# Splitting PSUM evacuation and chain copies between ScalarE and VectorE in a decode attention backward kernel

## The chip, the cores and the metric

One core of one Trainium2 chip. The time is the device time of one execution in microseconds, on the slowest (here the only) core. Every kernel was run next to the kernel before on the same chip, and its result was compared with the reference. "Before" and "after" are the two kernels; "span" is the length of the profiled execution, about 1.8 us less than its device time.

Engines: PE is TensorE, ACT is ScalarE, DVE is VectorE, POOL is GpSimd, SP is SyncE. To *evacuate* an outer product means to copy it from PSUM to an SBUF buffer as bf16, from where it is stored to DRAM.

## The reference, cut to what matters

```python
def _fwd(x, k_cache, v_cache, wq, wo, w_gate, w_up, w_down):
    xn = layernorm(x)                       # x: (2, 1, 576)
    q  = xn @ wq                            # 32 heads of 128, 16 KV heads
    p  = softmax(q . k_cache)               # k_cache, v_cache: (2, 16, 4096, 128) bf16
    o  = p . v_cache
    return x + o @ wo + ((B_x@w_gate) * (B_x@w_up)) @ w_down
# the outputs: the result and the gradients of all eight inputs of _fwd for grad_out
```

The caches and weights that must be read are 92.5 MB, and so are the gradients that must be written. The gradient of each cache is a sum of outer products: a row of `p` (or of `ds`, the gradient of the scores) times a short vector. 16 steps go over the caches; in each step, heads of K and V are loaded, K gives scores, V gives `dp`, a chain of small operations (called the *chain* here: `s_sb`, softmax, `ds`, `o_sb`) runs through all engines, and the outer products of the step before are made and stored.

## The kernel before

`# ...` marks a cut.

```python
def ps_m(shape):  return ps.tile(list(shape), FP32, tag="m",  bufs=2)      # PSUM, chains
def ps_sc():      return ps.tile([P, P], FP32,      tag="sc", bufs=2)      # PSUM, scores
def ps_o():       return ps.tile([P, 2, 512], FP32, tag="o",  bufs=2)      # PSUM, pairs of banks

load = {"v": 0.0, "s": 0.0}                 # a cost model, kept while the program is built
def evac(out, in_, cols):
    cv = 0.16 + cols * 0.00104
    cs = 0.19 + cols * 0.00083
    if load["v"] + cv < load["s"] + cs:
        load["v"] += cv
        nc.vector.tensor_copy(out=out, in_=in_)
    else:
        load["s"] += cs
        nc.scalar.copy(out, in_)
def dve(us): load["v"] += us                # other work of DVE, told to the model
def act(us): load["s"] += us

def build_bd(st, b, s, t):                  # block-diagonal operand of the outer products
    # ... two matmuls into bp
    nc.scalar.copy(dense[:], bp[:]);  act(0.4)
    bd = bds[n_bd[0] % 3];  n_bd[0] += 1
    for a in range(4):
        nc.gpsimd.tensor_copy(bd[32 * a:32 * a + 32, :, a, :], dense[32 * a:32 * a + 32])

def by_rows(t_ps):                          # in softmax and in dscores
    nc.scalar.copy(s_sb[:] ..., view(t_ps[:], ...));  act(0.35)
    nc.tensor.transpose(s_ps[:], s_sb[:], identf[:])

def contract(rowsT, heads):                 # p.V and ds.K
    # ... 64 matmuls into o_ps
    nc.scalar.copy(o_sb[:], o_ps[:]);  act(0.3)
    nc.tensor.matmul(t_ps[:], lhsT=o_sb[:], rhs=RV[:] ...)

def outer_units(rows, bd, b, l0, oview):    # eight units for a step's K, eight for its V
    def unit(x, cp):
        # ...
        o = ps_o()
        # ... two matmuls into o
        evac(view(st[:], ...), o[:].rearrange("p c (a d) -> p c a d", a=4), 1024)
        # ... a store of 1 MB after each fourth unit

def softmax(s_ps):
    s_ps = by_rows(s_ps)
    # ... maximum
    nc.scalar.activation(ex[:], s_ps[:], AF.Exp, bias=negb[:], scale=SCALE, accum_out=z[:])

# the last stage: the result, the gradient of x and the gradients of wq (stq, stqt) and wo (sto)
def prepare():
    # ... loads
    nc.vector.tensor_copy(x_f[:], x_b2[:])
    nc.vector.tensor_copy(dy_f[:], dy_b2[:])
    nc.vector.tensor_scalar(xn_f[:], x_f[:], mu[:], None, op0=ALU.subtract)
    nc.vector.tensor_scalar(xn_f[:], xn_f[:], rstd[:], None, op0=ALU.mult)
def gradient():                             # some ten DVE operations on 2 x 576, in a chain
    nc.vector.reduce_sum(m1[:], dxn, axis=AX.X)
    # ...
    nc.vector.tensor_add(dx_bf[:], t1[:], dy_f[:])
```

## Time and profile before

| | before |
|---|---|
| device time, median (range) of 3 runs | 504.05 us (503.95 to 505.25) |
| span of the profiled run, granted PE clock | 501.6 us, 0.879 |
| moved | 186.07 MB, 371 GB/s mean |

The prediction below shows the slices and stretches. From the page, the busy times, and from the table of the costliest groups the evacuations of `so`, the tiles of the cache gradients (columns: line, engine, operation, output and input, count; busy us, mean ns; idle time before them and what ended it), and the copies that build `bd`:

```profile
PE 398.5 (79%) x7417; PEld 266.4 (53%) x7417; DVE 352.5 (70%) x626; ACT 333.7 (67%) x488; POOL 254.2 (51%) x500
...
L112 ACT CAST so<-ps_o 128x1024 bf16<-128x1024 f32 x227 | 221.2, 1023 | 60.6 <-PE ps_o L93 54.2
...
L516 POOL COPY bd<-dense 32x256 bf16<-32x256 bf16 x128 | 50.7, 396 | 13.2 <-ACT dense L511 8.7
...
L109 DVE CAST so<-ps_o 128x1024 bf16<-128x1024 f32 x29 | 35.1, 1209 | 17.3 <-PE ps_o L93 14.3
```

No engine is full over the whole span. The cost model gives ACT nearly all evacuations already (227 of 256 for `so`), because DVE has the 128 big transposes, 155 us. So the change moves only the rest.

### The profile page before, as it was taken

Reading aid. Unit: us, or ns where it says so; the run is one execution under the profiler, and the core shown is the slowest. Engines: PE = TensorE matmul, PEld = TensorE weight load, DVE = VectorE, ACT = ScalarE, POOL = GpSimd, SP = SyncE. Lnnn points to the kernel's source line nnn. Section 1 sums busy time; section 2 is a strip of 40 time slices with the busy share of each in tenths; the row PEclk is TensorE's granted clock in tenths of the full one; section 3 lists DMA queues with packets and bytes.
Section 4 is the critical chain, followed back from the end, with each engine's and each line's share of the span. In section 5 each row is a group of like instructions: output and inputs, shape, how many; then the busy total and the mean of one; then the engine's idle time right before and its main releaser. Section 6 shows DMA issues by size and latency. Waiting matters only on the chain.

```text
span 501.6 us, 17288 instructions
## 1 busy us (share of the span) xinstructions
PE 398.5 (79%) x7417; PEld 266.4 (53%) x7417; DVE 352.5 (70%) x626; ACT 333.7 (67%) x488; POOL 254.2 (51%) x500
## 2 busy tenths in 40 slices
PE   2678838988988869877978889958898887888962
PEld 1565525666656536555645546535665545565520
DVE  6677643887877845856967776956787684899574
ACT  4244866857884775838746695857856685777763
POOL 5235354466546544554646355554656356383613
PEclk9877978979997878959998897979998897989985
DMA  8998999999999999999999999999999999994675
GB/s 253 387 401 293 346 417 322 422 416 409 401 419 407 417 416 330 418 417 408 348 378 398 395 419 364 392 416 393 394 350 417 408 418 398 394 375 175 229 268 211
DMA packets 52900, 186.07 MB, mean 371 GB/s; under 512 B 4140, under 2 KB 19128, under 8 KB 44632
## 3 DMA queue, kind: packets, MB, share of 16 engines
q1 hardware_dynamic: 28392, 92.49, 48.4%
q0 software_dynamic: 24432, 92.48, 46.6%
q8 instruction: 58, 0.95, 0.7%
q14 instruction: 18, 0.15, 0.1%
HBM read 92.48 MB, written 92.48 MB: 369 GB/s over the span
## 4 chain that ended last, share of the span: by engine, by line
PE 41%; ACT 18%; DMA 16%; DVE 13%; issue 6%; POOL 1%; POOLq 0%; DVEq 0%; ACTq 0%
PE ps_o L93 19%; ACT so L112 13%; PE ps_m L93 12%; DMA out_dram<-so 12%; PE ps_sc L93 7%; DVE X L121 5%; DMA kv<-in_A_k_cache_dram 4%; DVE so L109 2%; ACT sto L112 2%; DVE Xw L121 1%; DVE stq L109 1%; DVE stw L109 1%; PE ps_m L648 1%; PE ps_m L574 1%; PE ps_sc L552 1%
## 5 line engine op out<-in xcount | busy, mean ns | idle before, releaser
L112 ACT CAST so<-ps_o 128x1024 bf16<-128x1024 f32 x227 | 221.2, 1023 | 60.6 <-PE ps_o L93 54.2
L121 DVE STREAM_TRANSPOSE X<-kv 128x1024 f32<-128x1024 f32 x128 | 155.4, 1224 | 18.2 <-PE ps_sc L93 15.0
L600 POOL DMA_DIRECT2D out_dram<-so x64 | 49.7, 777 | 93.5 <-ACT so L112 33.5
L93 PEld LDWEIGHTS <-X 128*128 128x128 bf16 x2048 | 81.5, 103 | 26.4 <-DVE X L121 11.5
L93 PE MATMUL ps_o<-bd,prm 128*128 128x512 bf16 x256 | 83.7, 438 | 14.1 <-DVE stw L109 5.4
L93 PE MATMUL ps_sc<-W,X 128*128 128x64 bf16 (+1 forms) x2048 | 89.3, 200 | 4.6 <-DVE X L121 2.3
L93 PE MATMUL ps_o<-bd,dsm 128*128 128x512 bf16 x256 | 74.7, 382 | 14.5 <-ACT so L112 11.5
L516 POOL COPY bd<-dense 32x256 bf16<-32x256 bf16 x128 | 50.7, 396 | 13.2 <-ACT dense L511 8.7
L109 DVE CAST so<-ps_o 128x1024 bf16<-128x1024 f32 x29 | 35.1, 1209 | 17.3 <-PE ps_o L93 14.3
L93 PE MATMUL ps_m<-kv,rowT 128*32 128x128 bf16 x2048 | 44.6, 255 | 2.0 <-DVE cr L650 1.4
L93 PEld LDWEIGHTS <-prm 128*128 128x128 bf16 x256 | 22.7, 108 | 38.6 <-issue 27.9
L93 PEld LDWEIGHTS <-dsm 128*128 128x128 bf16 x256 | 21.3, 97 | 36.2 <-issue 26.1
L93 PEld LDWEIGHTS <-rowT 128*32 128x32 bf16 x2048 | 37.9, 115 | 4.7 <-issue 1.6
L496 POOL COPY W<-rep 32x16 bf16<-32x16 bf16 x128 | 24.9, 195 | 25.5 <-PE ps_sc L93 15.6
L112 ACT CAST stw<-ps_o 128x1024 bf16<-128x1024 f32 x27 | 26.8, 1035 | 16.1 <-DMA out_dram<-so 10.2
L580 POOL TENSOR_TENSOR prm<-pr,maskc 128x1024 bf16<-128x1024 bf16 x16 | 30.2, 1887 | 12.9 <-DVE pr L630 12.7
L580 POOL TENSOR_TENSOR dsm<-ds,maskc 128x1024 bf16<-128x1024 bf16 x16 | 30.3, 1894 | 12.1 <-DVE ds L651 11.4
L571 ACT COPY o_sb<-ps_m 128x128 f32<-128x128 f32 x32 | 8.6, 270 | 37.1 <-PE ps_m L93 37.0
L93 PE MATMUL ps_o<-hb,xnr 32*128 32x128 bf16 (+1 forms) x360 | 20.0, 238 | 15.9 <-ACT so L112 7.7
L93 PEld LDWEIGHTS <-xnr 32*128 32x128 bf16 (+1 forms) x440 | 14.3, 100 | 33.1 <-issue 29.1
L121 DVE STREAM_TRANSPOSE Xw<-wgu 128x1152 f32<-128x1152 f32 x18 | 24.6, 1369 | 4.6 <-PE ps_sc L93 4.6
L396 POOL DMA_DIRECT2D out_dram<-stw x18 | 13.7, 762 | 26.1 <-ACT stw L112 14.7
(179 smaller groups left out, 583.1 us busy)
## 6 DMA issues: line engine op xcount, KB each, us to landing
out_dram<-so POOLq DMA_DIRECT2D x64, 1024.0 KB, 11.3
kv<-in_A_k_cache_dram SPq DMA_DIRECT2D x32, 1024.0 KB, 13.9
kv<-in_A_v_cache_dram SPq DMA_DIRECT2D x32, 1024.0 KB, 15.2
out_dram<-stw POOLq DMA_DIRECT2D x18, 512.0 KB, 9.0
wd<-in_B_w_down_dram SPq DMA_DIRECT2D x9, 576.0 KB, 6.3
out_dram<-std POOLq DMA_DIRECT2D x9, 576.0 KB, 11.7
wo<-in_A_wo_dram SPq DMA_DIRECT2D x4, 1152.0 KB, 9.9
wgu<-in_B_w_gate_dram SPq DMA_DIRECT2D x9, 512.0 KB, 15.1
```

Source lines behind the costliest of these rows:

```text
L93: ins = nc.tensor.matmul(*args, **kwargs)
L109: nc.vector.tensor_copy(out=out, in_=in_)
L112: nc.scalar.copy(out, in_)
L121: nc.vector.transpose(out, in_)
L396: nc.gpsimd.dma_start(out[0:512, f0:f0 + FS].rearrange("(c p) n -> p c n", p=P), st[:])
L496: nc.gpsimd.tensor_copy(view(W[t][:], 32 * a, 32, 48 + 4 * a, [[2 * WW, 4], [WW + 2, 2], [1, 2]]), view(st["rep"][:], 32 * a, 32, t * 4 * ...
L516: nc.gpsimd.tensor_copy(bd[32 * a:32 * a + 32, :, a, :], dense[32 * a:32 * a + 32])
L552: nc.tensor.transpose(s_ps[:], s_sb[:], identf[:])
L571: nc.scalar.copy(o_sb[:], o_ps[:])
L574: nc.tensor.matmul(t_ps[:], lhsT=o_sb[:], rhs=RV[:].rearrange("p x r -> p (x r)"), start=True, stop=True)
L580: nc.gpsimd.tensor_tensor(m[:], view(rows[:], 0, P, 0, [[0, 8], [1, P]]), view(maskc[:], 0, P, 0, [[1, 8], [0, P]]), ALU.mult)
L600: nc.gpsimd.dma_start(oview[b, :, :, l0 + x].rearrange("a m n -> m a n"), st[:].rearrange("p a c d -> p a (c d)"))
```

## The change

Its intent: the four small copies of the chains stood in ACT's queue among evacuations of 1 us each, and some evacuations stood in DVE's queue among the chains. The change sorts them. ACT alone evacuates until the last chain, and DVE makes all copies of the chains. For the end it adds a third PSUM pair (two single banks of the scores' tag), lets both engines evacuate, prepares the last stage on GpSimd, and stores from free big buffers. The four GpSimd copies for `bd` become one product with a mask.

```diff
+    def ps_pair():
+        pairs_made[0] += 1
+        if ending and pairs_made[0] % 3 == 0:
+            o = [ps.tile([P, 512], FP32, tag="sc", bufs=2, name="ps_x") for _ in range(2)]
+            return [t[:] for t in o], None
+        o = ps_o()
+        return [o[:, 0, :], o[:, 1, :]], o
     def evac(out, in_, cols):
-        if load["v"] + cv < load["s"] + cs:
+        if ending and load["v"] + cv < load["s"] + cs:
-            nc.scalar.copy(gs[:], ug[:])
+            nc.vector.tensor_copy(gs[:], ug[:])
-        nc.scalar.copy(dense[:], bp[:])
+        nc.vector.tensor_copy(dense[:], bp[:])
-        bd = bds[n_bd[0] % 3]
-        n_bd[0] += 1
-        for a in range(4):
-            nc.gpsimd.tensor_copy(bd[32 * a:32 * a + 32, :, a, :], dense[32 * a:32 * a + 32])
+        bd = sb.tile([P, 2, 4, Dh], BF16, tag="bd", bufs=3, name=f"bd{t}")
+        nc.gpsimd.tensor_tensor(bd[:], view(dense[:], ...), view(maskq[:], ...), ALU.mult)
-        nc.scalar.copy(s_sb[:] ...            # and o_sb alike
+        nc.vector.tensor_copy(s_sb[:] ...
-                o = ps_o()                    # in the units of so, stq and sto
+                o, whole = ps_pair()          # a third pair is evacuated as two halves
+        stq = nat if g == NGRP - 1 else swtile
-            nc.vector.tensor_copy(x_f[:], x_b2[:])      # dy_f alike
+            nc.gpsimd.tensor_copy(x_f[:], x_b2[:])
-            nc.vector.tensor_scalar(xn_f[:], x_f[:], mu[:], None, op0=ALU.subtract)
-            nc.vector.tensor_scalar(xn_f[:], xn_f[:], rstd[:], None, op0=ALU.mult)
+            nc.gpsimd.tensor_scalar(xn_f[:], x_f[:], mu[:], rstd[:], op0=ALU.subtract, op1=ALU.mult)
+    ending.append(1)                          # after the chain of the last step
+    load["v"] = load["s"] = 0.0
```

(Cut: the access patterns of the half evacuations, the constant `maskq`, and the removed memsets of the three `bds`.)

More of the change, by code (lines that the diff above doesn't have):

```diff
@@ L81, in ps_o @@
         return ps.tile([P, 2, 512], FP32, tag="o", bufs=2, name="ps_o")
+    pairs_made = [0]
+    ending = []
+    def ps_pair():
[5 more added lines that the diff above has]
+        return [o[:, 0, :], o[:, 1, :]], o
     class Block:
@@ L112, in evac, with evac_pair @@
             nc.scalar.copy(out, in_)
+    def evac_pair(out, o, whole, cols, view_in=lambda t: t):
+        if whole is not None:
+            evac(out(None), view_in(whole[:]), cols)
+        else:
+            for a in range(2):
+                evac(out(a), view_in(o[a]), cols // 2)
     def dve(us):
@@ L151 @@
         nc.vector.reduce_sum(maskc[:], view(C32[:], 0, P, 0, [[1, 8], [8, 4]]), axis=AX.X)
+    maskq = const.tile([P, 4], BF16, name="maskq")
+    nc.vector.tensor_copy(maskq[:], Q4[:])
     mask8 = const.tile([P, 4, 2], FP32, name="mask8")
@@ L228 @@
         nc.gpsimd.memset(t[:], 0.0)
-    bds = [const.tile([P, 2, 4, Dh], BF16, name=f"bd{i}") for i in range(3)]
-    for r in bds:
-        nc.gpsimd.memset(r[:], 0.0)
-    n_bd = [0]
     nwm = [0]
@@ L510, in build_bd @@
         dense = sb.tile([P, 2, Dh], BF16, tag="dense", bufs=1, name="dense")
-        nc.scalar.copy(dense[:], bp[:])
+        nc.vector.tensor_copy(dense[:], bp[:])
         act(0.4)
-        bd = bds[n_bd[0] % 3]
-        n_bd[0] += 1
-        for a in range(4):
-            nc.gpsimd.tensor_copy(bd[32 * a:32 * a + 32, :, a, :], dense[32 * a:32 * a + 32])
+        bd = sb.tile([P, 2, 4, Dh], BF16, tag="bd", bufs=3, name=f"bd{t}")
+        nc.gpsimd.tensor_tensor(bd[:], view(dense[:], 0, P, 0, [[Dh, 2], [0, 4], [1, Dh]]),
+                                view(maskq[:], 0, P, 0, [[0, 2], [1, 4], [0, Dh]]), ALU.mult)
         return bd
@@ L547, in by_rows @@
         s_sb = small("s_sb", (P, P), FP32, 1)
-        nc.scalar.copy(s_sb[:].rearrange("p (a c m) -> p a c m", a=4, c=8),
-                       view(t_ps[:], 0, P, 0, [[4, 4], [16, 8], [1, 4]]))
+        nc.vector.tensor_copy(s_sb[:].rearrange("p (a c m) -> p a c m", a=4, c=8),
+                              view(t_ps[:], 0, P, 0, [[4, 4], [16, 8], [1, 4]]))
         act(0.35)
@@ L570, in contract @@
         o_sb = sb.tile([P, Dh], FP32, tag="o_sb", bufs=1, name="o_sb")
-        nc.scalar.copy(o_sb[:], o_ps[:])
+        nc.vector.tensor_copy(o_sb[:], o_ps[:])
         act(0.3)
@@ L591, in f @@
                 st = m["st"]
-                o = ps_o()
+                o, whole = ps_pair()
                 with Block() as mm:
                     for c in range(2):
-                        mm(o[:, c, :], lhsT=rows[:, 2 * cp + c, :], rhs=bd[:, x].rearrange("p a d -> p (a d)"),
+                        mm(o[c], lhsT=rows[:, 2 * cp + c, :], rhs=bd[:, x].rearrange("p a d -> p (a d)"),
                            start=True, stop=True)
-                evac(view(st[:], 0, P, 2 * cp * Dh, [[Dh, 2], [8 * Dh, 4], [1, Dh]]),
-                     o[:].rearrange("p c (a d) -> p c a d", a=4), 1024)
+                evac_pair(lambda c: view(st[:], 0, P, (2 * cp + (c or 0)) * Dh,
+                                         ([[Dh, 2]] if c is None else []) + [[8 * Dh, 4], [1, Dh]]), o, whole, 1024,
+                          lambda x: x.rearrange("p c (a d) -> p c a d" if whole is not None else "p (a d) -> p a d", a=4))
                 if cp == 3:
@@ L695, in f @@
                 if A == 0:
-                    m["st"] = swtile([P, 2, GH * P], "stq")
+                    m["st"] = stq([P, 2, GH * P], "stq")
                 st = m["st"]
-                o = ps_o()
+                o, whole = ps_pair()
                 with Block() as mm:
@@ L703, in f @@
                             d0 = (2 * k + dc) * P
-                            mm(o[:, aa, 256 * dc:256 * dc + 256], lhsT=xnr[32 * a:32 * a + 32, d0:d0 + P],
+                            mm(o[aa][:, 256 * dc:256 * dc + 256], lhsT=xnr[32 * a:32 * a + 32, d0:d0 + P],
                                              rhs=R[32 * a:32 * a + 32, 1].rearrange("p h d -> p (h d)"),
                                              start=True, stop=True)
-                evac(view(st[:], 0, P, 512 * A, [[256, 2], [GH * P, 2], [1, 256]]),
-                     o[:].rearrange("p a (d n) -> p a d n", d=2), 1024)
+                evac_pair(lambda aa: view(st[:], 0, P, 512 * A + 256 * (aa or 0),
+                                          ([[256, 2]] if aa is None else []) + [[GH * P, 2], [1, 256]]), o, whole, 1024,
+                          lambda x: x.rearrange("p a (d n) -> p a d n" if whole is not None else "p (d n) -> p d n", d=2))
                 if A == 1:
@@ L730, in f @@
                 if h2 == 0 and k == 0:
-                    m["so"] = swtile([P, 4, D], "sto")
-                o = ps_o()
+                    m["so"] = stq([P, 4, D], "sto")
+                o, whole = ps_pair()
                 with Block() as mm:
@@ L735, in f @@
                         a = 2 * A + aa
-                        mm(o[:, aa, 0:HD2], lhsT=R[32 * a:32 * a + 32, 0, h2, :],
+                        mm(o[aa][:, 0:HD2], lhsT=R[32 * a:32 * a + 32, 0, h2, :],
                                          rhs=dyr[32 * a:32 * a + 32, k * HD2:(k + 1) * HD2], start=True, stop=True)
-                evac(view(m["so"][:], 0, P, h2 * D + k * HD2, [[2 * D, 2], [1, HD2]]), o[:, :, 0:HD2], D)
+                so = m["so"]
+                evac_pair(lambda aa: view(so[:], 0, P, h2 * D + k * HD2 + 2 * D * (aa or 0),
+                                          ([[2 * D, 2]] if aa is None else []) + [[1, HD2]]), o, whole, D,
+                          lambda x: x[:, :, 0:HD2] if whole is not None else x[:, 0:HD2])
                 if h2 == 1 and k == 1:
@@ L798, in prepare @@
             x_f = m["x"] = fin([2, D], FP32, "x_f2")
-            nc.vector.tensor_copy(x_f[:], x_b2[:])
+            nc.gpsimd.tensor_copy(x_f[:], x_b2[:])
             dy_f = m["dy"] = fin([2, D], FP32, "dy_f")
-            nc.vector.tensor_copy(dy_f[:], dy_b2[:])
+            nc.gpsimd.tensor_copy(dy_f[:], dy_b2[:])
             xn_f = m["xn"] = fin([2, D], FP32, "xn_f2")
-            nc.vector.tensor_scalar(xn_f[:], x_f[:], mu[:], None, op0=ALU.subtract)
-            nc.vector.tensor_scalar(xn_f[:], xn_f[:], rstd[:], None, op0=ALU.mult)
+            nc.gpsimd.tensor_scalar(xn_f[:], x_f[:], mu[:], rstd[:], op0=ALU.subtract, op1=ALU.mult)
             m["rowf"] = fin([2, 2, D], FP32, "rowf")
```

## The prediction

> **What bounds the kernel now.** I read the page's slices first, then a table of stretches, then the timeline of each engine from 440 us on, then the waits. The slices divide the 501.6 us span into 40 parts of 12.54 us.
>
> ```profile
> DMA  8998999999999999999999999999999999994675
> GB/s 253 387 401 293 346 417 322 422 416 409 401 419 407 417 416 330 418 417 408 348 378 398 395 419 364 392 416 393 394 350 417 408 418 398 394 375 175 229 268 211
> ```
>
> For 36 slices (to 451 us) the DMA engines are full and move about 390 GB/s; the last four slices are half empty. So there are two stages: a bulk that the transfers bound, and a tail of 50 us that something else bounds. The stretches say what (columns: window, length, busy us of PE, PEld, DVE, ACT, POOL with instruction counts, granted clock, DMA share, GB/s):
>
> ```profile
> 400.00:425.00 25.00, 20.78 (x359) 13.17 (x352) 16.08 (x27) 19.00 (x29) 13.63 (x27) 0.84 1.02 413
> ...
> 440.00:450.00 10.00, 8.13 (x162) 6.17 (x165) 9.08 (x19) 7.11 (x12) 8.18 (x18) 0.83 1.00 390
> 450.00:460.00 10.00, 8.21 (x188) 5.86 (x177) 9.38 (x13) 7.18 (x11) 4.97 (x8) 1.00 0.47 165
> 460.00:470.00 10.00, 9.14 (x215) 6.66 (x215) 6.59 (x17) 8.10 (x14) 6.62 (x8) 1.00 0.57 213
> 470.00:480.00 10.00, 8.18 (x95) 3.16 (x93) 5.11 (x8) 7.69 (x8) 3.11 (x6) 1.00 0.75 281
> 480.00:490.00 10.00, 5.69 (x34) 1.95 (x36) 8.71 (x19) 5.65 (x8) 2.26 (x3) 0.82 0.65 246
> 490.00:501.60 11.60, 3.18 (x22) 0.73 (x19) 4.13 (x5) 3.18 (x4) 3.29 (x5) 0.50 0.58 204
> ```
>
> DVE is 92% busy from 440 to 460, while the DMA starves (165 GB/s): stage A, the last chains of scores. From 466 to 496 no engine is full: stage B, the last outer products, where PE and the evacuating engines wait for each other over two PSUM pairs. The last V load is issued at 425.24 us; loads of V land in a median of 15.2 us, so nothing but stores is left after about 440 us. The stores after 450 are 1.65+2.13+2.81+2.46+2.37 = 11.4 MB (GB/s times length), 28 us at 405 GB/s, against 51.6 us taken. So at most some 20 us are to be had in the tail; in the bulk only a few, in the dips.
>
> Stage A in detail, with the place where I expect most (start, length, engine, line, what):
>
> ```profile
> 449.10 0.64 DVE L801 CAST dy_f<-dy_b 2x576 f32<-2x576 bf16 x1
> ...
> 449.52 1.97 POOL L580 TENSOR_TENSOR dsm<-ds,maskc 128x1024 bf16<-128x1024 bf16 x1
> ...
> 449.67 2.13 DVE L803 TENSOR_SCALAR xn_f<-x_f,mu 2x576 f32<-2x576 f32 x1
> ...
> 451.73 1.21 DVE L109 CAST so<-ps_o 128x1024 bf16<-128x1024 f32 x1
> ...
> 452.99 0.59 PE L93 MATMUL ps_o<-bd,prm 128*128 128x512 bf16 x2 [1.59 <-DVE so L109]
> ```
>
> The preparation of the last stage sits on DVE in front of an evacuation, and PE stands still for 1.59 us because of it, with the last score matmuls behind it in its queue. L803 takes 2.13 us although L804, the same operation on the same shape, takes 0.50 us.
>
> Stage B: from 466.09 to 495.7 us there are 33 evacuations of outer products (19 of `so`, 8 of `sto`, 4 of `stq`, 2 of `stqt`) and two final uses of a pair, 0.85 us each. ACT alone, back to back, shows about 0.96 us per pair:
>
> ```profile
> 475.55 1.93 ACT L112 CAST so<-ps_o 128x1024 bf16<-128x1024 f32 x2 [0.68 <-PE ps_o L93]
> ```
>
> [...] L803 ends at 451.80, just after the GpSimd product ends at 451.49[...]. [...] the trace has 1023, and two in 1.93 us. [...] the trace has 1209. So DVE is the dearer evacuator by 0.19 us. [...] The GpSimd product of 128x1024 takes 1887 ns in this trace; no DVE twin is there to compare.
>
> **The change part by part.**
>
> Bulk evacuation. DVE has 61 evacuations in the whole kernel (29 `so` 35.1 us, 9 `stw` 10.8, 7 `stq` 8.4, 7 `sto` 5.2, 7 `stt` 2.9, 2 `stqt` 1.4: 63.8 us). Some 13 of them, about 13 us, fall in stage B. The other 51 us go to ACT, some 44 us there (1023/1209). In return DVE takes `dense` 12.7, `s_sb` 9.5, `o_sb` 8.6 and `gs` 3.4, 34.2 us. Before stage B ACT gains 44-33, about +11 us, and DVE loses some 17. ACT is then about 75% busy in the bulk, DVE 67%, PE still 80%. None becomes the bound, and the DMA is already full. I put the bulk at zero, give or take 3 us.
>
> Mask product. 128 GpSimd copies (4 x 396 ns = 1.58 us per build) become 32 products like `prm`, 1.89 us: +0.3 us each, +10 us of GpSimd in all, off the path (GpSimd 51% busy). The three first memsets (2.7 us) go; the first `bd` is wanted much later, so nothing.
>
> Stage A, 440 to 466.6 us. DVE busy 23.7 us. Leaving: `stw` 1.19, two `so` 2.38, `stt` 0.39, preparation 0.47+0.64+2.13+0.50 = 3.74; sum 7.7. Arriving: three `dense`, three `s_sb`, two `o_sb`, 2.7. Net 5 less: 18.7. ACT goes from 20.0 to about 21.3. PE has 22.2 and becomes the bound. From 26.6 us to about 24: **2.5 us** won, of which the 1.59 us stop is the part I can point to.
>
> Stage B, 29.6 us. PE's work, summed from its timeline, is some 21 us. ACT has 17.9 us and DVE 20.9, of which 9.3 are no evacuation. A third of the pairs come as two single-bank tiles with two evacuations, one more fixed cost of about 0.2 us each: some ten of those, +2 us. (17.9+20.9+2)/2 is about 20.5 each if shared evenly; the sharing does not see all of DVE's other work, so DVE nearer 23. The third pair takes away the waiting for a pair, but PE, ACT and DVE are in order and are all at 21 to 23, so I take 25 us: **4.5 us** won.
>
> Drain. The last issue is at 496.2 and the span ends 5.4 us later. Stores produced faster leave more queued: 0 to 1.5 us given back. I take **1 us** lost. The last `stq` and `sto` go to the free big buffers, so no wait for a store buffer comes in.
>
> Bulk dips: the DMA share is 0.55 and 0.77 from 45 to 55 us and 0.73 from 245 to 250. Chains that no longer queue behind evacuations could fill some of that: **1.5 us** won.
>
> Sum: 2.5+4.5-1+1.5 = 7.5 us. 504.05-7.5 is about **496.5 us**, 1.5% less.
>
> **The rivals.**
>
> Rival 1, convoy on DVE. The moved copies bring their waits along:
>
> ```profile
> ACT o_sb L571 <- PE ps_m L93: 37.0, 20, 4.9
> ...
> ACT gs L332 <- PE ps_m L93: 15.5, 5, 12.8
> DVE X L121 <- PE ps_sc L93: 15.0, 22, 2.7
> ```
>
> ACT stood 37 and 15.5 us at the head of its queue for these. If DVE stands there instead, the transposes behind it come late and PE's scores with them. For it: DVE is in order and 67% busy. Against it: PE is in order too, so what ACT waited for is mostly PE at other work, and in the bulk the DMA hides it. If it reaches stage A it eats the gain: 502 to 506 us.
>
> Rival 2, the bulk gains as well. Evacuation on DVE stops the transposes when store buffers are full (`stw` on DVE waited 15.9 us for stores, in three stops of up to 6.9). With ACT alone evacuating, only ACT stops, DVE and PE run on until the next pair is wanted, and compute is further along when the loads end, so the tail is shorter. Against it: PE meets an outer product after every half head, so it stops soon too, and such stops happen only where the DMA is full anyway. If it works: 486 to 491 us.
>
> Rival 3, stage B is held by the stores. From 466 us 8.5 MB go out; at 390 GB/s, 22 us. If issue comes in lumps of 1 MB, the last lumps queue and the gain of stage B falls to 2 us: 499 us.
>
> **Range and chances.** Main path 496.5; rival 2 pulls down by up to 10, rivals 1 and 3 up by 3 to 9. I give rival 2 in a notable degree 0.25, rival 1 0.2, rival 3 0.2. Range 488 to 503. The limit of 2% is 494.0 us: chance of faster 0.36, within 2% 0.60, slower 0.04; slower needs the convoy to make DVE the bound of the bulk, against full DMA.
>
> **What would show each step right or wrong.** Stage A: no wait of PE for an evacuation on DVE before the last scores, and the last dscores about 2.5 us earlier counted from the last load. Stage B: from the last contraction to the last evacuation 25 us instead of 29.6, ACT and DVE each over 75% busy, PE rarely waiting for a pair. Drain: last issue to the end 5.5 to 7 us. Bulk: DMA share 1.0, and 450 us reached with the same bytes moved within 1.5 MB; if far more has been moved, rival 2 is right. Rival 1 shows as waits of DVE on `o_sb` or `gs` of over 30 us in sum, together with longer waits of PE for `X`. The prediction is wrong if the bulk moves by more than 4 us either way, or if stage B stays above 28 us with three pairs.

L803 and the GpSimd product are those of the timeline, and nothing there shows that the one held the other; 1023 and 1209 are the mean ns of one evacuation of 128x1024 in the trace of before, on ACT (227 of `so`) and on DVE (29).

Three things that the prediction uses without a number, or without saying where the number is from, the traces show:

- That ACT, DVE and PE are "in order": work that is ready is seen standing behind work in front of it. On ACT of after, `ex` starts at 457.02 us though its last input is there at 450.2, behind eight evacuations. On DVE of after, an evacuation of `sto` starts at 482.94 us though PE's last matmul before it has ended by 479.02, behind the gradient of x. On PE of before, the score matmuls start at 453.56 us though the last `X` before them is done at 447.75, behind an outer product that waited until 452.99.
- The "fixed cost of about 0.2 us" of a second evacuation: in the trace of after, two evacuations of 128x512 take 0.23 us more than one of 128x1024 on ACT (624 ns each, 1021 for the whole) and 0.15 us more on DVE (686 each, 1224).
- The 405 GB/s at which the stores after 450 us would take 28 us: what before moved from 230 to 235 us. Up to 451.4 us its mean is 388.

## The result, and the profile after

| | before | after |
|---|---|---|
| device time, median (range) of 4 runs | 504.11 (503.95 to 505.25) us | 498.56 (498.15 to 501.1) us |
| ratio, 95% interval | 1 | 0.9896 (0.986 to 0.9932) |
| span of the profiled run, clock | 501.6 us, 0.879 | 496.4 us, 0.907 |

A ratio is the mean time of one kernel's fast runs over that of the other's of the same rounds, so not quite the ratio of the medians. Executions over 1.5% slower than the fastest of the same kernel are left out of the means. All outputs are right. The change gains 1.0%: within 2%, 2 us above the predicted 496.5.

The page after: busy times, the last two rows of the slices, and the groups that answer to those shown before.

```profile
PE 379.2 (76%) x7344; PEld 257.4 (52%) x7417; DVE 327.2 (66%) x680; ACT 348.4 (70%) x439; POOL 264.1 (53%) x404
...
DMA  8998999999899999999999999999999999996765
GB/s 256 384 394 304 378 415 390 422 421 407 303 393 356 407 414 360 419 419 412 401 422 407 417 421 346 413 372 353 409 420 411 417 418 372 415 372 240 264 260 190
...
L124 ACT CAST so<-ps_o 128x1024 bf16<-128x1024 f32 x249 | 238.6, 1021 | 70.3 <-PE ps_o L105 29.1
...
L532 POOL TENSOR_TENSOR bd<-dense,maskq 128x1024 bf16<-128x1024 bf16 x32 | 60.6, 1892 | 17.3 <-DVE dense L529 16.1
```

ACT has 15 us more and DVE 25 us less, as intended. (73 of the 7417 matmul records are missing from this trace, so PE's busy time isn't compared.) The mask products cost the 10 us of GpSimd that were predicted. The DMA row is full for 36 slices as before, but a slice is 12.41 us now, not 12.54, and the tail reads 6765 instead of 4675.

**Where the 5.2 us of span come from.** I read the same events from both traces: the landing of the last load, the last two executions of the operation that makes `ds` from `dp` (steps 15 and 16 of 16), the last copy `o_sb` (the end of the last chain), the last evacuation. Times in us from the span's start:

| event | before | after | after minus before |
|---|---|---|---|
| last load landed | 441.3 | 434.8 | -6.5 |
| `ds` of step 15 | 447.8 | 439.5 | -8.3 |
| last `o_sb` | 467.9 | 462.7 | -5.2 |
| last evacuation ends | 495.7 | 489.2 | -6.5 |
| span | 501.6 | 496.4 | -5.2 |

So all of the gain is there before the end begins, and by the `ds` of step 15 there were 3 us more. The last chain gives 3.1 us back (20.1 us from the `ds` of step 15 to the last `o_sb` before, 23.2 after). From there to the end of the span both kernels take 33.7 us: the measures for the end, on which the prediction put its largest term, gain nothing in sum. Three questions follow: what gained in the bulk, what lost in the last chain, and why the end stands still.

**The bulk, in the waits.** What DVE waited for, and PE for the transposed heads `X` (line, releaser: us in all, times, longest), lines picked from the view of after:

```profile
DVE rz L645 <- PE ps_m L643: 17.5, 7, 10.1
DVE X L141 <- DMA kv<-in_A_k_cache_dram: 13.6, 8, 7.4
DVE o_sb L588 <- PE ps_m L105: 10.6, 13, 2.5
PE ps_sc L105 <- DVE X L141: 9.9, 16, 3.7
DVE gs L350 <- PE ps_m L105: 6.6, 7, 1.4
```

and, from that of before, what answers to three of them:

```profile
DVE rz L627 <- PE ps_m L625: 4.4, 3, 2.8
DVE X L121 <- DMA kv<-in_A_k_cache_dram: 3.2, 3, 1.5
PE ps_sc L93 <- DVE X L121: 2.3, 7, 0.7
```

The waits on `o_sb` and `gs` came along as rival 1 said, but they are 17 us in sum where ACT had 52.5, under the 30 us that the prediction set as the mark. Two waits of DVE have grown: that for the sum of the exponentials (`rz`), 17.5 us where it had 4.4, and that of the transposes for K to land, 13.6 us where it had 3.2. The second half of rival 1's sign came too: PE waits 9.9 us for `X`, 2.3 us before. None of these lines says what gained; the shared kernel below waits for K as long and gains nothing. The dips of DMA that the prediction named have filled in part: 294 to 321 GB/s in 40 to 60 us, 339 to 411 in 240 to 255 us.

**The last chain, in the timelines of ACT and DVE of after** (start, length, engine, line, what; in brackets the idle time before and its releaser):

```profile
449.73 7.43 ACT L124 CAST so<-ps_o 128x1024 bf16<-128x1024 f32 x8 [0.24 <-PE ps_o L105]
457.02 0.41 ACT L641 ACTIVATE ex<-ps_sc,negb 128x128 f32<-128x128 f32 x1
```

```profile
450.09 0.08 DVE L635 DVE_READ_ACCUMULATOR2_ANT negb<- 128x1 f32 x1
...
457.55 0.29 DVE L661 CUSTOM_DVE_ANT_0 ds<-ex,ps_sc 128x128 bf16<-128x128 f32 x1 [5.92 <-ACT ex L641]
```

The last exponential stands behind eight evacuations in ACT's queue: its last input, `negb`, is there at 450.2 us, it starts at 457.02, and DVE stands still for 5.92 us. The stretches show the reversal against the page before, where DVE was full here (columns as in the prediction):

```profile
450.00:460.00 10.00, 7.59 (x96) 3.52 (x99) 3.65 (x13) 10.00 (x13) 6.50 (x7) 1.00 0.69 249
460.00:470.00 10.00, 9.25 (x205) 5.45 (x197) 4.06 (x10) 8.07 (x11) 6.33 (x6) 1.00 0.64 241
470.00:480.00 10.00, 6.38 (x49) 2.46 (x49) 7.33 (x17) 6.44 (x11) 2.55 (x4) 1.00 0.73 275
```

ACT is busy 10.00 of 10 us from 450 to 460, DVE 3.65. From 470 on, no engine is full, as before.

**The end, in the timelines of PE, DVE and ACT of after:**

```profile
483.43 0.39 PE L105 MATMUL ps_x<-dyr,R 32*128 32x288 bf16 x1 [4.41 <-DVE sto L121]
```

```profile
478.46 0.73 DVE L858 TENSOR_REDUCE m<-rowf 2x1 f32<-2x576 f32 x1
...
482.26 0.75 DVE L873 TENSOR_TENSOR dx_bf<-t,dy_f 2x576 bf16<-2x576 f32 x1
482.94 0.44 DVE L121 CAST sto<-ps_x 128x288 bf16<-128x288 f32 x1
```

```profile
484.10 0.64 ACT L124 CAST sto<-ps_o 128x576 bf16<-128x576 f32 x1 [4.23 <-PE ps_o L105]
```

The whole chain of the gradient of x, 478.46 to 483.0 us, stands in DVE's queue in front of the evacuations of `sto`. All three pairs are then full, PE waits 4.41 us and ACT 4.23. I call this the hole. It is not in the kernel before, where four of DVE's `sto` evacuations (486.33 to 490.28) lie between the operations of the gradient chain (484.93 to 490.95).

### The profile page after: what moved, and what is told of

The parts are those of the page before. It is cut to its first block, busy times and chain, and to the rows that moved or that the text cites. A ratio compares the mean times of both kernels' runs of the same rounds, so it can differ in the third digit from the quotient of the medians.

```text
span 496.4 us, 16989 instructions
## 1 busy us (share of the span) xinstructions
PE 379.2 (76%) x7344; PEld 257.4 (52%) x7417; DVE 327.2 (66%) x680; ACT 348.4 (70%) x439; POOL 264.1 (53%) x404
## 4 chain that ended last, share of the span: by engine, by line
DMA 34%; PE 25%; ACT 12%; DVE 11%; issue 7%; POOL 5%; POOLq 0%; ACTq 0%; DVEq 0%
DMA out_dram<-so 22%; PE ps_o L105 10%; ACT so L124 10%; DMA kv<-in_A_k_cache_dram 7%; PE ps_m L105 7%; DVE X L141 6%; DMA kv<-in_A_v_cache_dram 5%; PE ps_sc L105 4%; POOL bd L532 2%; ACT std L124 1%; DVE Xw L141 1%; POOL prm L597 1%; PE ps_m L591 1%; DVE dense L529 1%; ACT sto L124 0%
## 5 line engine op out<-in xcount | busy, mean ns | idle before, releaser
L124 ACT CAST so<-ps_o 128x1024 bf16<-128x1024 f32 x249 | 238.6, 1021 | 70.3 <-PE ps_o L105 29.1
L141 DVE STREAM_TRANSPOSE X<-kv 128x1024 f32<-128x1024 f32 x128 | 157.4, 1232 | 41.2 <-DMA kv<-in_A_k_cache_dram 13.6
L105 PE MATMUL ps_o<-bd,prm 128*128 128x512 bf16 x212 | 69.0, 396 | 13.8 <-ACT so L124 6.1
L532 POOL TENSOR_TENSOR bd<-dense,maskq 128x1024 bf16<-128x1024 bf16 x32 | 60.6, 1892 | 17.3 <-DVE dense L529 16.1
L124 ACT CAST stw<-ps_o 128x1024 bf16<-128x1024 f32 x36 | 34.4, 1019 | 15.6 <-PE ps_o L105 12.0
L124 ACT CAST std<-ps_o 128x576 bf16<-128x576 f32 x36 | 21.3, 648 | 27.7 <-PE ps_o L105 22.9
L105 PE MATMUL ps_m<-kv,rowT 128*32 128x128 bf16 x2048 | 37.5, 228 | 2.0 <-issue 1.7
L105 PEld LDWEIGHTS <-dsm 128*128 128x128 bf16 x256 | 22.2, 105 | 29.9 <-issue 22.8
L105 PEld LDWEIGHTS <-rowT 128*32 128x32 bf16 x2048 | 31.1, 101 | 6.9 <-issue 4.4
L124 ACT CAST sto<-ps_o 128x576 bf16<-128x576 f32 x27 | 16.5, 650 | 14.1 <-PE ps_o L105 12.8
L105 PEld LDWEIGHTS <-Wdy 128*128 128x128 bf16 x306 | 20.7, 103 | 9.0 <-issue 3.2
```

The costliest lines, as they stand in the source:

```text
L105: ins = nc.tensor.matmul(*args, **kwargs)
L141: nc.vector.transpose(out, in_)
L532: nc.gpsimd.tensor_tensor(bd[:], view(dense[:], 0, P, 0, [[Dh, 2], [0, 4], [1, Dh]]), view(maskq[:], 0, P, 0, [[0, 2], [1, 4], [0, Dh]]), ...
```

## The experiments

Twelve kernels in three calls. The kernel before was run with each call: median 504.33 us (first call), 503.57 (second), 505.45 (third, 502.53 to 508.04). Single runs of one kernel spread by up to 7.7 us and follow the granted clock to a degree: within kernels, over these 75 runs, 0.01 more clock goes with 1.9 us less (correlation -0.54). The mean clock is 0.88 for the kernel before and 0.89 to 0.90 for most others. Whether that is a cause or a consequence of a better order isn't settled; a higher clock is not enough for a gain, for the kernel with shared evacuation below has 0.892 and the time of before. But after has 0.892 too, on average over its four runs, so by that slope some 2 of its 5 us may go with the clock (an estimate); no run separates them. So differences of times under some 2 us decide nothing here, and I lean on events inside the traces beside the ratios. Of the twelve expectations three hold in neither branch: the copies back on ACT (505 us at most, measured 529.88), the end alone (505 at most, measured 506.29) and the late outer products (490 to 494.5, measured 496.44). Three more are missed by 1 us or less.

The end of the last chain to the end of the span is called the *end* below; both original kernels have 33.7 us.

### Which half of the bulk gains

**Evacuation shared by the cost model all along; everything else as after.**

```diff
-        if ending and load["v"] + cv < load["s"] + cs:
+        if load["v"] + cv < load["s"] + cs:
```

> The changed kernel, but outer products shared between ACT and DVE by the cost model all along, as before; the copies of the chains stay on DVE. Theory M with 'DVE free of evacuations' as its cause: last load lands at 439 to 442 us and the time is 502 to 505 us. Theory E, or a gain from another part: 497 to 500 us.

Measured: 504.98 us (502.38 to 508.25), ratio to before 1.0016 (0.9966 to 1.0066). The whole gain is gone; the `ds` of step 15 comes at 449.2 us, not at 439.5. The copies on DVE alone gain nothing.

Two things that looked like the gain are here without it. The last load lands at 437.0 us, 4.3 us earlier than before, and DVE waits for K as in after:

```profile
DVE X L141 <- DMA kv<-in_A_k_cache_dram: 16.4, 5, 6.1
```

So the landing doesn't measure the gain. The `ds` of step 15 follows it better: it comes at 437.8 to 442.3 us in the ten kernels of this document where ACT evacuates alone in the bulk and DVE makes `s_sb`, and at 447.8 to 449.2 us in the three that share the evacuation.

**The four copies of the chains back on ACT; everything else as after.**

```diff
-        nc.vector.tensor_copy(o_sb[:], o_ps[:])      # and gs, dense, s_sb
+        nc.scalar.copy(o_sb[:], o_ps[:])
```

> The changed kernel with the copies of the chains (dense, s_sb, o_sb, gs; 34 us) back on ACT, which still evacuates alone until the end. If only the freeing of DVE counts: 497 to 500 us. If ACT must be relieved in turn (it would be 383 us busy of some 500): 501 to 505 us, loads landing 3 us later or more.

Measured: 529.88 us (525.38 to 531.72), ratio 1.0493 (1.0436 to 1.055): 5% slower than before. From its table of waits:

```profile
DVE ds L661 <- PE ps_sc L569: 57.5, 9, 12.7
```

and from that of before:

```profile
DVE ds L643 <- PE ps_sc L552: 8.4, 5, 6.8
```

`ds` needs the transposed `s_sb`. It waits 57.5 us, up to 12.7 at once; before, 8.4 us. ACT is busy 373.0 us in it, 71% of its span, and DVE 57%, so ACT isn't full on average; the reading is that the copy stands in the queue behind evacuations, and these wait for pairs and store buffers. The next run tests it. A part of the loss may be clock (0.861 on average over its four runs).

**As the last, but `s_sb` alone on DVE** (`gs`, `dense` and `o_sb` on ACT).

> e4 (ACT evacuates alone, copies of the chains on ACT: 529.9 us) with s_sb alone given to DVE. If the chain of scores, which waits on s_sb (DVE waited 57.5 us for the transpose behind it in e4), is what made e4 slow: 498 to 505 us. If it is ACT's load (its busy time falls by 9.5 us of 373): 522 to 528 us.

Measured: 497.77 us (497.06 to 498.68), ratio 0.9877 (0.9845 to 0.9909). One copy of 0.27 us, 32 times (8.7 us of DVE in all), takes back the 32 us and is worth as much as all four. `s_sb` is on the way from the scores to the exponential and from `dp` to `ds`, and these are what the next products and stores hang on; the other three can stay on ACT at no cost that the runs show. Whether another single copy moved would have done the same was not run. In this kernel ACT is busy 74% of its span (366.3 us; 71%, 373.0 us, in the one that lost 32 us), and still waits 14.5 us for `gs`.

With the run of the next section (sharing and ACT copies, with the end measures: 506.29 us) these make a square: shared and copies on ACT 506, shared and copies on DVE 505, ACT alone and copies on ACT 530, ACT alone and copies on DVE 498.6. Neither half gains by itself; the first alone loses. This is shown for the times. Why sharing costs what it does is shown only in part: the waits of DVE for store buffers (18.3 us for `stw` and `so` before) are 4.0 us in the shared kernel, so they are not the reason that I had given. That an evacuation in DVE's queue stands in front of transposes and chains in the same way as on ACT fits, but no run isolates it.

### The bulk alone, the end alone

**The end measures alone** (sharing all along, copies on ACT, four GpSimd copies as before; third pair, reset balance, GpSimd preparation and free store buffers kept).

> Before, with the measures for the end alone (third pair, balance reset in the end, preparation on GpSimd, big buffers for the last stq and sto); bulk as before (outer products shared, copies of the chains on ACT, four copies on GpSimd). If the end measures are worth what the third pair alone took away in e1 (about 3 us) plus the preparation: 500 to 502 us with the dscores of the last step but one at 446 to 450 us as before (447.8). If they are worth nothing without the bulk part: 503 to 505 us.

Measured: 506.29 us (505.07 to 507.87), ratio 1.0047 (1.0006 to 1.0088). It has the hole of 4.41 us; its end takes 34.6 us.

**The bulk alone**: no third pair, preparation on DVE, old store buffers, four GpSimd copies.

```diff
-        if ending and pairs_made[0] % 3 == 0:
+        if False and pairs_made[0] % 3 == 0:
-        stq = nat if g == NGRP - 1 else swtile
+        stq = swtile                         # and prepare() and build_bd() as before
```

> The bulk part alone: ACT alone evacuates until the last chain, DVE makes the four copies, both share in the end; no third pair, last stage prepared on DVE, old store buffers, four GpSimd copies. Theory (the bulk gains about 6.5 us up to the last load by itself, and without the third pair it loses part of that in the last outer products, as the kernel without the third pair did at 501.8): last load landed at 434 to 437 us, total 500 to 503. Rival (the measures at the end are what make the bulk's gain reach the end at all): 504 us, as before, with the last load still landing by 437. Second rival (part of the early landing comes from the end measures or from the mask product): last load landed at 439 us or later.

Measured: 499.01 us (496.16 to 503.6), ratio 0.989 (0.9833 to 0.9946), as good as the whole change. The last load lands at 437.4 us (in a profiled run of 501.48, one of its slower ones). Its end takes 33.5 us with two pairs. There is no hole. Its timeline of DVE:

```profile
482.90 0.73 DVE L121 CAST sto<-ps_o 128x576 bf16<-128x576 f32 x1
483.57 0.50 DVE L873 TENSOR_SCALAR t<-rowf,m 2x576 f32<-2x576 f32 x1
483.99 0.63 DVE L875 TENSOR_SCALAR t<-xn_f,m 2x576 f32<-2x576 f32 x1
484.55 0.73 DVE L121 CAST sto<-ps_o 128x576 bf16<-128x576 f32 x1
```

Evacuations and gradient operations alternate. Together: bulk alone 0.989, end alone 1.0047, both 0.9896. The gain is the bulk's; no gain of the rest of the change shows in the sum.

### Why the end stands still

**Without the third pair**, everything else as after (the first line of the diff above).

> The changed kernel without the third PSUM pair; both engines still evacuate in the end. Theory M (the gain of 5.5 us was made before the last load landed, 434.8 against 441.3 us, and the end gave nothing net): 498 to 500 us. Theory E (the third pair and the sharing in the end are worth several us, the earlier loads are an accident of order): 501 us or more, stage B (last contraction to last evacuation) over 3 us longer than the 30 us of the changed kernel.

Measured: 501.76 us (501.12 to 505.01), ratio 0.9962 (0.9921 to 1.0002). This is on the side of theory E: from the end of the last contraction to the last evacuation it takes 31.7 us, 26.6 in after. Its end takes 37.6 us, and it has a hole of 3.31 us:

```profile
488.22 0.42 PE L105 MATMUL ps_o<-dyr,R 32*128 32x288 bf16 x2 [3.31 <-DVE sto L121]
```

**The cost model told of DVE's work in the last stage**, so that it gives the evacuations beside that work to ACT:

```diff
             nc.sync.dma_start(out_0.rearrange("b s d -> (b s) d"), o0_bf[:])
+            dve(1.6)
             nc.vector.tensor_add(t0, t0, view(gp[:], 0, 2, 512 + P, [[160, 2], [1, 32]]))
+            dve(1.2)
             nc.sync.dma_start(out_1.rearrange("b s d -> (b s) d"), dx_bf[:])
+            dve(4.7)
```

> The changed kernel with the last stage's DVE work (output 1.6, rows 1.2, gradient 4.7 us) entered into the balance of the end, so that evacuations next to it go to ACT. If the 4.41 us stop of PE behind the gradient on DVE costs the end what it seems to: the stop under 2 us and 494.5 to 497 us. If stores or other work fill the gap: 498 to 499 us.

Measured: 493.57 us (492.75 to 497.59), ratio 0.9806 (0.9752 to 0.9861). Its end takes 30.8 us. PE, at the place of the hole:

```profile
477.26 0.30 PE L105 MATMUL ps_o<-dyr,R 32*128 32x288 bf16 x2 [0.24 <-ACT sto L124]
477.56 0.70 PE L105 MATMUL ps_x<-dyr,R 32*128 32x288 bf16 x2
478.41 0.96 PE L105 MATMUL ps_o<-dyr,R 32*128 32x288 bf16 x4 [0.15 <-ACT sto L124]
```

PE waits 0.24 and 0.15 us where it waited 4.41. With the last two kernels and the bulk alone the end fits one table (us from the last `o_sb` to the end of the span):

| | hole | no hole |
|---|---|---|
| two pairs | 37.6 (no third pair) | 33.5 (bulk alone) |
| third pair | 33.7 (after) | 30.8 (gradient seen) |

The third pair is worth 2.7 to 3.9 us and the hole costs 2.9 to 4.1 us. The change brought both, so they cancelled. (Each cell is one trace, and the kernels in it differ in other parts of the end too; the 37.6 us are of a run of 505.01 us, the slowest of its kernel. The other traces with a third pair agree: the seven kernels with third pair and hole have ends of 32.5 to 35.0 us; the three whose cost model is told of DVE's work, leaving out the one with late outer products, have 30.1 to 30.8. The kernel before, two pairs and no hole, has 33.7.) What brought the hole isn't isolated. It stays at 4.41 us with the preparation on DVE, with four copies for `bd`, with the copies of the chains on ACT and with sharing all along, and at 3.31 us without the third pair. The one measure that all kernels with the hole have and the bulk alone has not is the free store buffers, but that was not run by itself.

**The last stores of wq's and wo's gradients issued from SyncE instead of GpSimd**, on top of the last kernel:

```diff
-                nc.gpsimd.dma_start(out_4[...], ...)                                   # and out_5
+                (nc.sync if g == NGRP - 1 else nc.gpsimd).dma_start(out_4[...], ...)
```

> The kernel whose cost model sees the gradient chain (493.6 us), with the last group's stores of its two weight gradients issued from SyncE instead of GpSimd. Theory (the last issues, 1.1 to 1.4 us each in one row on GpSimd, lengthen the drain of 7.4 us): drain 6 us or less and 491.5 to 492.5 us. Rival (the bytes still queued set the drain): within 1 us of 493.6, drain still about 7 us.

Measured: 494.56 us (493.66 to 499.21), ratio 0.9817 (0.9772 to 0.9863). No gain: from the last evacuation (488.0 us) to the end of the span (495.1) it takes 7.1 us, 7.4 without. (The 1.1 and 1.4 us of the expectation are rows of two issues each in the trace of "gradient seen", 1.11 and 1.42 us, so 0.56 and 0.71 us an issue.) The issues on GpSimd are not what the drain waits for. The run also repeats the gain of the told cost model on another chip: its end takes 30.6 us.

### The last chain

**The last exponential with fewer evacuations in front of it**: as "gradient seen", but in the last step no outer products are issued with the second K head.

```diff
-            K.append(slot(kview, 0, b, l0 + x, s_ps, per, ...))
+            K.append(slot(kview, 0, b, l0 + x, s_ps, per, ...,
+                          0 if x == 1 and n + 1 == NIT else 2))     # units per half head
```

> e2 (the last stage's DVE work seen by the balance), and in the last step no outer products are issued with the second K head, so that 4 instead of 8 evacuations stand in front of the last exponential on ACT. If the 5.92 us wait of DVE for the exponential lengthens the end: the wait 2 to 3 us, the last dscores 3 us earlier, 490 to 492 us. If the evacuations that come later then lengthen the end by as much: 493 to 494.5 us, as e2 (493.57).

Measured: 496.44 us (495.13 to 498.36), ratio 0.985 (0.9803 to 0.9896). Its timelines of ACT and DVE:

```profile
450.08 3.77 ACT L124 CAST so<-ps_o 128x1024 bf16<-128x1024 f32 x4 [0.24 <-PE ps_o L105]
453.75 0.37 ACT L641 ACTIVATE ex<-ps_sc,negb 128x128 f32<-128x128 f32 x1
```

```profile
454.24 0.29 DVE L661 CUSTOM_DVE_ANT_0 ds<-ex,ps_sc 128x128 bf16<-128x128 f32 x1 [2.26 <-ACT ex L641]
```

Four evacuations instead of eight stand in front, the wait falls from 5.92 to 2.26 us, and from the `ds` of step 15 to the last `o_sb` it takes 19.4 us instead of 23.5 in its parent. But the end then takes 35.9 us instead of 30.8, as the evacuations that were put off come later; 1.2 us of that are a longer drain. The time does not improve on the 493.57 of its parent. This fits that the 3 us lost in the last chain are mostly evacuations done early, not time lost; one trace of each kernel doesn't show more.

**Preparation on DVE**, everything else as after.

> The changed kernel with the last stage prepared on DVE as before (four operations, 3.74 us in the trace of before). If the preparation was on the path, as the prediction has it for before: 500 to 502 us, and DVE stops over 1.5 us between the scores of the last step. If DVE has slack there now, because it no longer evacuates and waits 5.9 us for the exponential anyway: 498 to 499.5 us, no different from the changed kernel.

Measured: 500.45 us (503.17, 496.76, 497.78, 503.13), ratio 0.9925 (0.9856 to 0.9993). The profiled run, one of the two long ones, shows on DVE, PE and GpSimd:

```profile
443.65 2.84 DVE L827 TENSOR_SCALAR xn_f<-xn_f,rstd 2x576 f32<-2x576 f32 x1
446.42 0.27 DVE L588 COPY o_sb<-ps_m 128x128 f32<-128x128 f32 x1
```

```profile
446.75 0.59 PE L591 MATMUL ps_m<-RV,o_sb 128*128 128x4 f32 x2 [2.25 <-DVE o_sb L588]
```

```profile
443.50 0.75 POOL L414 DMA_DIRECT2D out_dram<-stw  x1 [0.56 <-ACT stw L124]
444.26 1.90 POOL L597 TENSOR_TENSOR dsm<-ds,maskc 128x1024 bf16<-128x1024 bf16 x1
```

L827 takes 2.84 us, from 443.65 to 446.49; its twin of the same shape takes 0.49. A store's issue on GpSimd runs from 443.50 to 444.25 and a product from 444.26 to 446.16, and the copy `o_sb` behind L827 is late. It looks like L803 of the kernel before, 2.13 us beside a GpSimd product from 449.52 to 451.49. But L827 starts 0.61 us before the product, and only 0.15 us after the store's issue; no run isolates what held either, and that it costs time in the end is not shown. In this run the `ds` of step 15 is level with after (440.0 to 439.5) and the last one 5.5 us later (464.6 to 459.1), but two other runs of the kernel are as fast as after, and the spread is that of the bulk alone. Its end, 33.3 us, is as after.

### The mask product, and the best version

**Four GpSimd copies instead of the product**, everything else as after.

> The changed kernel with the mask product on GpSimd undone: four GpSimd copies per block-diagonal tile, as before. Theory (the product is off the path; it only adds 10 us of GpSimd work in all): 498 to 500 us, within 1.5 us of the changed kernel's 498.6. Rival (the longer single instruction on GpSimd delays the outer products[...]): 496 us or less. Second rival (one instruction instead of four, and three fixed buffers no longer shared, is part of the gain of the bulk): 501 us or more.

Measured: 499.93 us (497.3 to 504.65), ratio 0.9901 (0.9846 to 0.9955), as after. 10 us of GpSimd more or less make no difference that shows.

**`s_sb` alone on DVE, and the cost model told of DVE's work**: the two gains put together.

> Only s_sb copied on DVE (dense, o_sb and gs stay on ACT), and the cost model told of DVE's work in the final stage (1.6, 1.2 and 4.7 us) as in the run that saw the gradient chain. Theory (the two are independent: s_sb on DVE alone gives 497.8, telling the cost model gave 5 us): 492 to 495 us. Rival (with the three other copies on ACT, ACT is the fuller engine in the end and the shift of evacuations to it gives nothing): 496 to 498 us.

Measured: 493.79 us (490.02 to 497.72, the last slow), ratio of the four fast runs 0.9737 (0.9688 to 0.9786). It is 2.6% faster than before and the best of all, with an end of 30.1 us. Whether it also beats "gradient seen" (0.9806, 0.9752 to 0.9861) is open: the intervals overlap.

## Why the prediction was right or wrong

The total and the class were right; the sum that led there was wrong in most of its terms, and the errors cancelled: the bulk was put 5.0 us too low and the two stages together 7.0 us too high. That the total came within 2 us was luck. By its own sign ("the bulk moves by more than 4 us either way") the prediction was wrong, counted by the last load. The terms, with what the trace of after shows for each (bulk: landing of the last load; the two stages: to the end of the last contraction on PE, and from there to the last evacuation):

| term | predicted gain | measured |
|---|---|---|
| bulk | 1.5 us | 6.5 us |
| stage A | 2.5 us | -1.5 us |
| stage B | 4.5 us | 1.5 us |
| drain | -1 us | -1.3 us |
| sum | 7.5 us | 5.2 us |

Two readings in the prediction are off. Of DVE's evacuations 11 fall in stage B (11.6 us), not 13. And its stage B starts at 466.09 us, while the last contraction runs from 466.53 to 467.61: from its end, before takes 28.1 us, not 29.6, and after 26.6. Its limit of 28 us for stage B is kept, but decides little, as before is hardly over it.

**Bulk: the term was mis-sized.** (The 6.5 us are the landing of the last load, a loose measure, as the shared kernel lands at 437.0 us without a gain.) The prediction read the DMA share of 1.0 as proof that engine order can't matter, and put only the dips down as a gain. By 440 us after has moved 1.2 MB more (171.92 to 170.72 MB, from the sizes of the landed packets), 3 us at some 400 GB/s (slices 33 to 36 of before, 401 to 451 us, have 375 to 418); by 450 us, the prediction's mark, 0.4 MB (174.99 to 174.62), inside the 1.5 MB that it allowed. What is ahead is rather the order of the work: at 430 us after has 2.0 MB more of loads and 0.8 MB less of stores behind it, and the chain of step 15 is 8.3 us ahead. So rival 2 was right in direction: the bulk gained 5 us more than its term, close to the least that rival 2 stood for (496.5 down to 491), though the total did not follow. The loss of the whole gain in the shared kernel shows that ACT evacuating alone is needed for it, and the kernel with all copies on ACT that it isn't enough. Rival 2's named mechanism, full store buffers stopping DVE, was not what the shared kernel showed. That no engine becomes the bound, that the mask product costs 10 us of GpSimd off the path, and that ACT gains and DVE loses busy time were right.

**Stage A: the step failed.** "PE has 22.2 and becomes the bound" counted busy time per engine. ACT was to be at 21.3 us of 24. It was in fact busy 26.0 of the 27.8 us between the last load and the end of the last contraction, and full from 450 to 460, with the exponential of the chain behind eight evacuations. Counted from the last load, the last `ds` came 1.2 us later (24.3 to 23.1), not 2.5 earlier. The change moved the chains' copies off ACT but left `ex` there, and the prediction passed over it. The PE stop for the preparation did go, as predicted: from 440 to 462 us the longest wait of PE is 0.49 us. The run that takes the wait down to 2.26 us gains no time in total, which fits that this loss is mostly work done early.

**Stage B: one step was missing.** The third pair is worth 2.7 to 3.9 us in the traces, not far under the 4.5 that stood for all of stage B. ACT and DVE were to be over 75% busy there and are at 63% and 71% (16.7 and 18.8 of 26.6 us). The prediction even says that "the sharing does not see all of DVE's other work", but turned it into a load, "DVE nearer 23". It is an order: the unseen gradient chain goes in one piece in front of the evacuations on which all three pairs hang. Telling the cost model gained the 2.9 us of the end in the trace and 0.9% in the ratio (0.9896 to 0.9806; the intervals meet at 0.986, but the repeat with SyncE has 0.9817).

**Drain** was right in size; that it is not the issue on GpSimd is shown by the SyncE run. **Rival 1** (a convoy on DVE) was rightly given little: 17.2 us of waits, not 30, and no loss in total, though PE's waits for `X` did grow. **Rival 3** (stores hold stage B) named nearly the numbers that came (a gain of 2 us in stage B, 499 us), but not the cause: in "gradient seen" it takes 23.3 us from the last `o_sb` to the last evacuation, 27.8 before and 26.6 after, with the same stores.

**The preparation, and the load of the engines.** L803 and L827 took 2.13 and 2.84 us, where the other operation of the same shape beside each took 0.50 and 0.49; what held them isn't isolated, and the runs can't show it to cost time. On GpSimd, in after, the two are one operation of 2.29 us, and the casts of 2x576 take 0.66 us each, 0.47 and 0.64 on DVE before. In the kernel with the copies back on ACT no engine was full on average (DVE 57%, ACT 71%), and yet 32 us hung on which of the two had one copy of 0.27 us (529.88 to 497.77 us).

## What to carry to other kernels

Where an engine's queue holds both long and urgent work, sort it by what hangs on it, not only by load: keep the one copy on the way from scores to exponential (here `s_sb`) out of the queue that evacuates, and move the others only if it costs nothing. A balance kept by a cost model must be told of every piece of other work, above all of chains near the end; telling it three numbers gave about as much again as the whole change (0.9896 to 0.9806). When a change has parts for the bulk and for the end, run each alone: here the sum was right while two parts of the end cancelled.
